# Another order of work, keys turned by 128-key block, and expert numbers cast on VectorE, in an attention, MLP and mixture-of-experts kernel

## The chip, the cores and the metric

The kernel runs on one core of a Trainium2 chip. The metric is the device time of one execution in microseconds (us), taken as the median of several runs. The engines have these names in the rows: PE (TensorE, matmuls), PEld (its weight loads), DVE (VectorE), ACT (ScalarE), POOL (GpSimd) and SP (SyncE, which issues most of the DMAs).

## The reference

Three stages follow one another; each takes the output of the one before.

1. Attention in chunks: 4 batches, 8 heads, 768 positions, head size 64. Each chunk of 32 queries sees 8 memory keys, 16 keys to the left, its own 32 and 8 to the right: 64 keys in all.
2. A dense layer on the 3072 tokens: `h = x @ w_in` (512 to 2048), `g = h * tanh(softplus(h))`, `g @ w_out` (2048 to 512).
3. A mixture of 8 experts: each token goes to the one expert whose embedding is the nearest by cosine, and gets `gate * (relu(x @ w1[e]) @ w2[e])`, with 1024 inner columns.

```python
scores = scale * np.matmul(q_c, k_full.transpose(0, 1, 3, 2))
out[:, :, c_start:c_end] = np.matmul(a, v_full)
...
g = h * np.tanh(sp)
return (g @ w_out).astype(np.float32)
...
expert_idx = np.argmax(logits, axis=1)
h = np.maximum(x[mask] @ w1[e], 0.0)
out[mask] = gate_w[mask, None] * (h @ w2[e])
```

## The kernel before, in words

**Matmuls.** Each fp32 product is split into a high and a low part and takes three matmuls (high by high, low by high, high by low). Splitting costs one cast (helper `split`, whose copy is recorded at L334) and one subtraction.

**The plan.** Nothing is issued where it is written. Every piece of work is a job of a list scheduler, `Plan`: a job names the engines that may do it with a modelled time (`on`), what it comes after (`after`), the buffers that it takes or uses (`get`, `use`) and a rank; the table NUDGE (L102) shifts the ranks of whole kinds of jobs. The plan then writes one instruction stream per engine, and each engine works through its own strictly in that order. So a stream is fixed before the launch, and an instruction that has to wait holds back all that stands behind it on its engine.

**Attention** works on 24 pairs of 64-query blocks, 6 pairs per batch. A pair P loads its queries (`load_q`) and its keys in two pieces: `load_k1` (104 rows: 8 memory keys and 96 keys) and `load_k2` (72 rows), both through helper `dma` (L319) on SP. `turn` (L511) transposes them on PE, 4 matmuls for each of the queries (128 rows, p_qT), the first key piece (104 rows, p_kT) and the second (72 rows, p_k). The copies `kT(0)` and `kT(1)` then lay the turned keys out as 4 chunks of 64 keys in a tile kT (5 copies in all, on ScalarE or VectorE). `S_` (L554, L559) multiplies them with the queries, then come the softmax, its transposition PT (L602) and the product with the values (p_X, L621).

**The dense layer** runs beside attention, since it needs only finished tokens: 128 steps, each a `p_h` of 12 matmuls (L732) and a `p_y` of 9 (L778). Attention's small PE jobs stand between these. The activation takes a chain of ScalarE and VectorE operations per step (L736 to L769).

**The experts.** `routing` works in two groups: group 1 takes the first 21 tiles of 128 tokens, while the dense layer still runs; group 2 takes the rest. A group gives tables of token places (p_tab, L1218), from which come the gather indices `gi` (L1232) and scatter indices, and the list of the expert numbers `ef`, in fp32. `numbers` (L1175) casts that list to integers, `ei`, on GpSimd, after the first two gathers of the group (L1288, issued on GpSimd too). Units of 256 tokens (pairs) or 128 (singles) then follow: units 0 to 2 are group 1's, the others group 2's. For each unit SP reads its expert's number into a register (L1302, and L1304 for the flag that says whether the weights must be fetched) and issues 8 weight loads of 512 KB (L1314): 4 of w1, then 4 of w2. The loads are split into ehi and elo; the gathered tokens are turned (`x_T`, L1331) and split into xs; `p_h` (L1395, 24 matmuls for each of the 4 chunks of a pair), the rectifier (hh), `p_y` (L1485), a scale and a scatter (L1511) end the unit. The weight tiles are two sets, used by units in turn.

Two lines set what the loads wait for:

```python
job(("experts", g), numbers, {G: 200}, rank=rk, after=[ex] + [("issue", "gather", first, a) for a in range(2)])
...
after = [("experts", g)] + ([("slo", u - 2, second, c)] if u >= 2 else [])
```

Nothing sets the order between the loads of one unit and those of the next but their ranks.

Of the kernel before, what the change touches and what calls it, by code (L numbers as in the profile page):

```python
# [38 lines left out]
HALF = KFF // 2  # L39
LEAVE = 2  # L40
# [46 lines left out]
def between(a, b):  # L87
# [15 lines left out]
    acta0=-0.6, acta1=-1.74, acta2=50.36, actb0=-1.76, actb1=-96.54, actb2=-81.79, actb3=-42.59, att00=40.88,  # L103
    att01=6.03, att02=-14.41, att03=12.63, att04=-3.12, att05=6.33, att06=-6.99, att07=-18.03, att10=10.46, att11=7.93,
    att12=-2.03, att13=-0.28, att14=-5.39, att15=28.34, att16=0.19, att17=-11.65, att20=7.04, att21=-2.49, att22=6.84,
    att23=0.68, att25=11.02, att26=-13.24, att27=2.06, att30=-0.41, att31=-70.31, att32=-0.58, att33=-1.39,
    att35=-0.38, att36=-1.67, att37=-67.52, att40=0.45, att41=-0.43, att42=13.06, att43=-2.17, att44=-38.4,
    att45=12.86, att46=9, att47=-2.37, att50=-1.08, att51=-18.11, att52=-6.46, att53=252.42, att54=-0.22, att55=-3.21,
    att56=-1.09, att57=2.56, att60=-5.29, att61=2.16, att63=-69, att64=-3.49, att65=145.06, att66=-0.33, att67=-14.14,
    att70=-0.37, att71=-329.92, att72=0.25, att73=-193.55, att74=-10.54, att75=-2.18, att76=-1.27, e00=-1.37, e01=8.52,  # L110
    e10=3.1, e11=23.17, e20=-86.99, e21=1, e30=0.07, e31=1.64, e40=10.43, e41=28.57, e50=1.56, e51=-2.1, e60=-22.39,
    e61=17.86, e70=-0.44, e71=-5.41, em=3.37, en0=24.71, en1=-0.52, en2=4.38, en3=27.95, en4=-27.14, en5=-7.94,
# [168 lines left out]
def attn_moe_moe_kernel(ctx, tc, q, k, v, mem_k, mem_v, w_in, w_out, emb, tau, w1, w2, cst, out, ydbg=None):  # L281
# [143 lines left out]
    def pairs(P):  # L425
# [39 lines left out]
        def load_k1(e):  # L465
# [5 lines left out]
            if spare or i == 0:  # L471
                dma(e, t[0:NMEM], mem_k[b].rearrange("h p d -> p h d"))
# [34 lines left out]
        def turn(name, src, rows):  # L507
            def f(e):
# [6 lines left out]
                if name == "kT":  # L515
                    tl["kT", P] = own(ktt, [128, J, 4, SEEN], "kT", bufs=1)
# [1130 lines left out]
```

## Time and profile before

| what | value |
|---|---|
| median of 3 runs | 1021.76 us (1020.55 to 1022.34) |
| the profiled execution | 1021.15 us |
| its span, first to last instruction | 1019.4 us |
| mean granted TensorE clock | 0.991 of full |
| instructions in the trace | 22817 |

The span is cut off at the first and last instruction, so the profiled execution's own time is 1.75 us longer. In a timeline or a chain each row begins with a time in us from the start of the span. A bracket at a row's end gives the idle time of its engine before it, and what ended that. A row of a chain says what the end waited for at that time. The tile names stand as out<-in.

### The profile page before, as it was taken

How to read it: one execution, taken by the hardware profiler on the slowest of the kernel's cores; microseconds unless marked ns; L12 is line 12 of the kernel's file. 1: busy time of each engine (PE TensorE's matmuls, PEld its weight loads, DVE VectorE, ACT ScalarE, POOL GpSimd, SP SyncE). 2: the span in 40 equal slices, each digit the busy share in tenths (PEclk: the TensorE clock that was granted, in tenths of full speed). 3: DMA queues.
4: the chain of work that ended last, by engine and by line, in shares of the span. 5: the costliest groups of instructions: out<-in, count | busy, mean ns of one | idle time of the engine just before them, and what ended most of it. 6: DMA issues, size and time to landing. Idle time of an engine off the chain costs nothing.

```text
span 1019.4 us, 22817 instructions
## 1 busy us (share of the span) xinstructions
PE 991.5 (97%) x8575; PEld 879.2 (86%) x8575; DVE 809.0 (79%) x1799; ACT 648.8 (64%) x1534; POOL 189.5 (19%) x142
## 2 busy tenths in 40 slices
PE   7899999999999999999999999999989999999997
PEld 6678888898888888888888899888979988988986
DVE  4889999669899869769869867979948667777972
ACT  4788888776877777778777767757424334443431
POOL 5000100000000000000000000011136455555742
PEclk9989999999999999999999999999989999999999
DMA  9997661233645234325313100089089868467300
GB/s 181 253 237 200 168 184 45 59 128 97 184 132 135 74 78 134 84 46 145 84 25 122 30 20 20 1 272 327 32 279 371 280 229 296 150 218 246 127 29 23
DMA packets 171817, 146.36 MB, mean 144 GB/s; under 512 B 105114, under 2 KB 134410, under 8 KB 171444
## 3 DMA queue, kind: packets, MB, share of 16 engines
q1 hardware_dynamic: 164868, 128.53, 43.5%
q0 software_dynamic: 5104, 15.89, 4.6%
q8 instruction: 69, 1.13, 0.5%
q10 hardware_dynamic: 1728, 0.43, 0.3%
q14 instruction: 48, 0.39, 0.1%
HBM read 137.11 MB, written 16.53 MB: 151 GB/s over the span
## 4 chain that ended last, share of the span: by engine, by line
PE 76%; DVE 8%; DMA 7%; issue 5%; POOL 2%; SPq 1%; ACT 0%; POOLq 0%; DVEq 0%
PE p_h L732 23%; PE p_y L778 23%; PE p_y L1485 10%; PE p_h L1395 9%; DMA eraw<-in_moe_w_dram 2%; PE p_h L1429 2%; DMA kn<-in_k_dram 2%; PE p_X L621 2%; PE p_S L559 2%; POOL elo L1367 1%; SPq L319 1%; PE p_PT L602 1%; PE p_xT L1331 1%; PE p_qT L511 1%; DMA qn<-in_q_dram 1%
## 5 line engine op out<-in xcount | busy, mean ns | idle before, releaser
L732 PE MATMUL p_h<-xt,win_h 128*128 128x384 f32 x1024 | 268.9, 344 | 0.6 <-DVE rn L761 0.5
L732 PEld LDWEIGHTS p_h<-xt,win_h 128*128 128x128 f32 x1024 | 185.3, 191 | 10.2 <-DVE rn L761 1.8
L732 PE MATMUL p_h<-xt,win_l 128*128 128x384 f32 x512 | 173.9, 340 | 0.0
L334 ACT CAST ehi<-eraw 128x1024 fp32r<-128x1024 f32 x89 | 92.9, 1049 | 120.0 <-PE p_y L1485 67.7
L778 PE MATMUL p_y<-wout_h,gh 128*128 128x512 f32 x384 | 157.1, 409 | 0.0
L778 PE MATMUL p_y<-wout_h,gl 128*128 128x512 f32 x384 | 151.9, 396 | 0.0
L778 PE MATMUL p_y<-wout_l,gh 128*128 128x512 f32 x384 | 151.8, 395 | 0.0
L1367 DVE TENSOR_TENSOR elo<-eraw,ehi 128x1024 fp32r<-128x1024 f32 x89 | 127.9, 1444 | 28.3 <-ACT ehi L334 27.7
L1485 PE MATMUL p_y<-ehi,hh 128*128 128x512 f32 x432 | 144.1, 400 | 0.0
L1395 PE MATMUL p_h<-xs,ehi 128*128 128x256 f32 x704 | 128.3, 283 | 7.0 <-DVE xs L1348 2.5
L755 ACT ACTIVATE m<-m,cf 128x384 f32<-128x384 f32 x128 | 79.1, 618 | 70.6 <-DVE m L751 69.7
L1395 PEld LDWEIGHTS p_h<-xs,ehi 128*128 128x128 f32 x704 | 110.4, 191 | 10.3 <-DVE xs L1348 2.7
L1367 POOL TENSOR_TENSOR elo<-eraw,ehi 128x1024 fp32r<-128x1024 f32 x39 | 94.9, 2432 | 81.1 <-DVE ehi L334 36.6
L851 DVE SCALAR_TENSOR_TENSOR junk<-ysb,en 128x512 f32<-128x512 f32 x144 | 99.0, 688 | 3.0 <-DMA ysb<-y_d 2.7
L1395 PE MATMUL p_h<-xs,elo 128*128 128x256 f32 x352 | 99.3, 282 | 0.0
L732 PEld LDWEIGHTS p_h<-xt,win_l 128*128 128x128 f32 x512 | 97.4, 190 | 0.0
L1485 PEld LDWEIGHTS p_y<-ehi,hh 128*128 128x128 f32 x432 | 80.9, 188 | 18.2 <-DVE hh L1454 0.3
L751 DVE SCALAR_TENSOR_TENSOR m<-sq,rn 128x384 f32<-128x384 f32 x128 | 71.0, 555 | 31.1 <-ACT rn L324 29.8
L758 DVE SCALAR_TENSOR_TENSOR rn<-m,rn 128x384 f32<-128x384 f32 x128 | 71.5, 558 | 30.0 <-ACT m L755 27.9
L736 ACT ACTIVATE sq<-p_h 128x384 f32<-128x384 f32 x128 | 62.8, 491 | 41.2 <-PE p_h L732 40.8
L778 PEld LDWEIGHTS p_y<-wout_h,gl 128*128 128x128 f32 x384 | 72.2, 188 | 17.3
L1485 PE MATMUL p_y<-elo,hh 128*128 128x512 f32 x216 | 85.2, 394 | 0.0
(264 smaller groups left out, 1770.8 us busy)
## 6 DMA issues: line engine op xcount, KB each, us to landing
eraw<-in_moe_w_dram SPq DMA_DIRECT2D x128, 512.0 KB
en<-en_d SPq DMA_DIRECT2D x48, 256.0 KB
vn<-in_v_dram SPq DMA_DIRECT2D x162, 56.0 KB
raw<-in_moe_w_in_dram SPq DMA_DIRECT2D x16, 512.0 KB
raw<-in_moe_w_out_dram SPq DMA_DIRECT2D x16, 512.0 KB
y_d<-ysb SPq DMA_DIRECT2D x24, 256.0 KB
qn<-in_q_dram SPq DMA_DIRECT2D x22, 256.0 KB
ysb<-y_d SPq DMA_DIRECT2D x18, 256.0 KB
```

Source lines behind the costliest of these rows:

```text
L334: (nc.scalar.copy if e == A else nc.vector.tensor_copy)(out, src)
L559: nc.tensor.matmul(ps[s][r:r + CHUNK, h, n // 2, :], a[64 * s:64 * s + 64, n, QB * h + CHUNK * x:QB * h + CHUNK * x + CHUNK], c[64 * s:64 ...
L732: nc.tensor.matmul(p, w, xt[j][:, a, kk, :], start=(n == 0), stop=(n == len(ops) - 1))
L736: nc.scalar.activation(t, tl["h", s], AF.Tanh, scale=0.5)
L751: nc.vector.scalar_tensor_tensor(t, tl["sq", s], 4.0, tl["rn", s], ALU.add, ALU.mult)
L755: nc.scalar.activation(t, t, AF.Square, bias=c15)
L758: nc.vector.scalar_tensor_tensor(tl["rn", s], tl["m", s], 0.75, tl["rn", s], ALU.add, ALU.mult)
L778: nc.tensor.matmul(yp[yh][t], x[:, c], w[g][:, o, :], start=(first and n == 0), stop=(final and n == 2))
L851: nc.vector.scalar_tensor_tensor(junk, tl["yio", t][:, 1], 1.0, tl["en", j, x], ALU.mult, ALU.mult, accum_out=lg[:, i, x:x + 1])
L1367: engs[e].tensor_sub(tl["elo", j], raw[b, second, c], tl["ehi", j].bitcast(F32))
L1395: nc.tensor.matmul(p[:, o, :], w[:, kk, s], v[:, kk, :], start=(kk == 0 and m == 0), stop=(kk == KDM - 1 and m == 2))
L1485: nc.tensor.matmul(tl["yy", u][a], v[:, kk, s], w[:, k, :], start=(kk == 0 and m == 0), stop=(kk == KEF - 1 and m == 2))
```

## The change

- **Keys.** From pair 6 on (`CARRY = 6`) a pair loads only its 128 new keys, in one piece, and turns them in one go of 128 rows. The 24 first keys of its window (8 of memory, 16 of the left) are kept: `keep` copies the last 16 from the previous pair's kT tile, which is now one tile for all; the first pair of a batch (6, 12, 18) loads 24 rows and turns these apart. `fresh_keys` lays out the rest with 2 copies. All of these, the turn too, come after `S` of the previous pair.
- **Expert numbers.** `numbers` runs on VectorE, and no longer after the group's first gathers.
- **Loads.** A unit's first weight load is issued after the last one of the unit before it.
- **Order.** NUDGE has new values, so that all work but the first loads and projections stands in another order.

By instructions: the turns p_k of 72 rows go from 96 matmuls to 24 and those of 104 rows from 88 to 16; 72 of 128 rows and 12 of 32 rows are new. Everything else on PE keeps its count. The new numbers of NUDGE are cut here to a line or two.

```diff
--- before.py
+++ after.py
...
+CARRY = 6
...
 NUDGE = dict(
-    acta0=-0.6, acta1=-1.74, acta2=50.36, actb0=-1.76, actb1=-96.54, actb2=-81.79, actb3=-42.59, att00=40.88,
...
+    acta0=-0.6, acta1=-1.51, acta2=-13.73, acta3=-199.64, actb0=-1.9, actb1=-983.54, actb2=-220.88, actb3=-519.98,
...
+        carry, start = P >= CARRY, P >= CARRY and i == 0
+        KB = NMEM + PREV
...
+            if carry:
+                get_keys(e, t, 0, w + PREV, w + PREV + 2 * QB)
+                return
...
+            if carry:
+                dma(e, t[0:NMEM], mem_k[b].rearrange("h p d -> p h d"))
+                get_keys(e, t, NMEM, w, w + PREV)
+                return
...
-                if name == "kT":
+                if name == "kT" and not carry:
...
+        def keep(e):
+            if P == CARRY:
+                tl["kTs"] = own(ktt, [128, J, 4, SEEN], "kT", bufs=1)
+            t = tl["kT", P] = tl["kTs"]
+            if i == 0:
+                p = tl["T", "k2", P]
+                copy(e, t[:, :, 0, 0:KB], p)
+                x = p[:, :, 0:NMEM]
+                copy(e, t[:, :, 1:4, 0:NMEM], bass.AP(tensor=x.tensor, offset=x.offset, ap=[x.ap[0], x.ap[1], [0, 3], x.ap[2]]))
+            else:
+                copy(e, t[:, :, 0, NMEM:KB], t[:, :, 3, SEEN - PREV:])
+
+        def fresh_keys(e):
+            t, p = tl["kT", P], tl["T", "kT", P]
+            copy(e, t[:, :, :, KB:], p.rearrange("p j (c n) -> p j c n", c=4))
+            x = p[:, :, CHUNK - PREV:CHUNK]
+            copy(e, t[:, :, 1:4, NMEM:KB], bass.AP(tensor=x.tensor, offset=x.offset, ap=[x.ap[0], x.ap[1], [CHUNK, 3], x.ap[2]]))
...
+            if start:
+                plan.dma(("k2", P), load_k2, size=rows(KB), rank=L(0.05), after=[("issue", "q", P)], get=[(k2t, k2s)], **iss(2))
+            plan.dma(("k1", P), load_k1, size=rows(128), rank=L(0.1), after=[("issue", "k2" if start else "q", P)], get=[("kn", ks)], **iss(2 if i == NQB - 2 else 1))
...
-        qh, kt, xb = ("qT", P), ("kT", P), [("X", P, a) for a in range(2)]
...
-        job(("Tk", P, 0), turn("kT", "kn", K1), {E: 350}, rank=R(0), after=[("k1", P)], use=[kh], get=[("a", t2), (ktt, kt)])
-        job(("Tk", P, 1), turn("k2", "kn2", K2), {E: 250}, rank=R(0), after=[("k2", P)], use=[k2s], get=[("a", t3)])
...
+        else:
+            if start:
+                job(("Tk", P, 1), turn("k2", "kn2", KB), {E: 290}, rank=R(0), after=[("k2", P), ("S", P - 1)], use=[k2s], get=[("a", t3)])
+            job(("Tk", P, 0), turn("kT", "kn", 128), {E: 436}, rank=R(0), after=[("k1", P), ("S", P - 1)], use=[kh], get=[("a", t2)])
...
+        if not carry:
+            job(("kT", P, 0), kT(0), {A: 750, V_: 900}, rank=R(1), after=[("Tk", P, 0)], use=[t2, kt])
+            job(("kT", P, 1), kT(1), {A: 430, V_: 530}, rank=R(1), after=[("Tk", P, 1)], use=[t3, kt])
+        else:
+            job(("kT", P, 1), keep, {A: 420, V_: 400} if start else {A: 160, V_: 115, G: 250}, rank=R(1), after=[("S", P - 1)] + ([("Tk", P, 1)] if start else [("kT", P - 1, 0)]),
+                get=[(ktt, kt)] if P == CARRY else [], use=([t3] if start else []) + ([] if P == CARRY else [kt]))
+            job(("kT", P, 0), fresh_keys, {A: 830, V_: 1000}, rank=R(1), after=[("Tk", P, 0), ("kT", P, 1), ("S", P - 1)], use=[t2, kt])
...
                 c = slice(first, u1 if g == 1 else NUNIT)
-                nc.gpsimd.tensor_copy(ei[:, c], ef[:, c])
-
-            job(("experts", g), numbers, {G: 200}, rank=rk, after=[ex] + [("issue", "gather", first, a) for a in range(2)])
+                nc.vector.tensor_copy(ei[:, c], ef[:, c])
+
+            job(("experts", g), numbers, {V_: 80}, rank=rk, after=[ex])
...
                 after = [("experts", g)] + ([("slo", u - 2, second, c)] if u >= 2 else [])
+                if u and c == 0 and second == 0:
+                    after.append(("issue", "ld", u - 1, 1, NC_ - 1))
...
-                put_job(("ld", u, second, c), load(second, c), dict(SP=470), base - 7 + 1.5 * second + 0.3 * c, after,
+                put_job(("ld", u, second, c), load(second, c), dict(SP=470 + (0 if c or second else 950 if u < 2 else 1450)), base - 7 + 1.5 * second + 0.3 * c, after,
                         [(f"w{8 * b + 4 * second + c}", h)] if u < 2 else [], [] if u < 2 else [h], dma=2 ** 19)
```

Three places in the streams follow. In the changed kernel, lines stand 2 to 46 further down: L511 is L522, L559 is L588, L732 is L776, L778 is L822, L1175 is L1219, L1288 is L1332, L1314 is L1358.

**PE, a pair in the middle of attention.** p_qT, p_kT and p_k are the turns of the queries and of the keys; the rows of p_h and p_y belong to the dense layer. Before, two turns of keys stand apart, each between a `p_h` and a `p_y`:

```order
L732 MATMUL p_h<-xt,win_h 128x384 x2
L732 MATMUL p_h<-xt,win_l 128x384
L511 MATMUL p_kT<-cf,kn 128x104 x4
L778 MATMUL p_y_6604<-wout_h,gh 128x512
...
L511 MATMUL p_k_7188<-cf,kn 128x72 x4
L778 MATMUL p_y_6604<-wout_h,gh 128x512
L778 MATMUL p_y_6604<-wout_l,gh 128x512
```

After, one turn of 128 rows follows directly on the previous pair's S:

```order
L588 MATMUL p_S<-kT,qT 32x64 x32
L522 MATMUL p_kT<-cf,kn 128x128 x4
L822 MATMUL p_y_6576<-wout_h,gh 128x512
...
L822 MATMUL p_y_6578<-wout_h,gl 128x512
L522 MATMUL p_qT<-cf,qn 128x128 x4
L776 MATMUL p_h<-xt,win_h 128x384 x2
```

The second key turn (72 rows) is gone, and the first now has 128 rows and stands behind S instead of behind a `p_h`.

**POOL and VectorE, the expert numbers.** vn are the gathered tokens, ei the integer numbers, out_dram<-yo the scatters. Before, on POOL, both casts stand behind gathers:

```order
L594 TENSOR_TENSOR pr<-pr,sm 128x256 x5
L1288 DMA vn<-y_d,gi 128x512 x2
L1175 CAST ei<-ef 1x3
L1288 DMA vn<-y_d,gi 128x512 x4
L1511 DMA out_dram<-yo,si 3072x512 x4
L1288 DMA vn<-y_d,gi 128x512 x2
L1175 CAST ei<-ef 1x20
L1367 TENSOR_TENSOR elo<-eraw,ehi 128x1024
```

After, on VectorE, the second group's cast stands directly behind the last step of the list (ra<-ra 1x3), ahead of the places' copy (ra<-p_tab) and of gi:

```order
L1252 TENSOR_TENSOR rhs_9581<-rhs_9581,ra 128x3x32
L1210 TENSOR_TENSOR ra<-ra 1x1
L1252 TENSOR_TENSOR rhs_9585<-rhs_9585,ra 128x3x32
L1211 CAST ra<-ra 1x3
L1252 TENSOR_TENSOR rhs_9587<-rhs_9587,ra 128x3x32
L1219 CAST ei<-ef 1x20
L1274 COPY ra<-p_tab 128x96
L1252 TENSOR_TENSOR rhs_9589<-rhs_9589,ra 128x3x32
L1275 SCALAR_TENSOR_TENSOR ra<-ra 128x32
L1413 TENSOR_TENSOR elo<-eraw,ehi 128x1024
L1276 CAST gi<-ra 128x32
```

The cast moved from behind four scatters and two gathers on POOL to the end of the list's own arithmetic on VectorE.

**SP, the first expert loads.** `TENSOR_LOAD ei` begins a unit; loads from w1 are the chunks that `p_h` needs, loads from w2 those of `p_y`. Rows of register moves (ISA) are left out at the dots. Before, the second unit begins behind one load of the first, and the two take turns (eraw_9093, 9108, 9144 and 9166 are the first unit's, the others the second's):

```order
L1314 DMA eraw_9093<-in_moe2_w1_dram 128x4x256
L1302 TENSOR_LOAD ei_102
...
L1314 DMA eraw_9106<-in_moe2_w1_dram 128x4x256
...
L1314 DMA eraw_9108<-in_moe2_w1_dram 128x4x256
...
L1314 DMA eraw_9133<-in_moe2_w1_dram 128x4x256
...
L1314 DMA eraw_9144<-in_moe2_w1_dram 128x4x256
...
L1314 DMA eraw_9164<-in_moe2_w1_dram 128x4x256
...
L1314 DMA eraw_9166<-in_moe2_w1_dram 128x4x256
...
L1314 DMA eraw_9169<-in_moe2_w1_dram 128x4x256
```

After, the first unit's eight loads stand together, w1 and then w2, ahead of the second unit's:

```order
L1346 TENSOR_LOAD ei_102
...
L1358 DMA eraw_8742<-in_moe2_w1_dram 128x4x256
...
L1358 DMA eraw_8773<-in_moe2_w1_dram 128x4x256
...
L1358 DMA eraw_8789<-in_moe2_w1_dram 128x4x256
...
L1358 DMA eraw_8796<-in_moe2_w1_dram 128x4x256
...
L1358 DMA eraw_8801<-in_moe2_w2_dram 128x2x512
...
L1358 DMA eraw_8806<-in_moe2_w2_dram 128x2x512
...
L1358 DMA eraw_8823<-in_moe2_w2_dram 128x2x512
...
L1358 DMA eraw_8831<-in_moe2_w2_dram 128x2x512
L1346 TENSOR_LOAD ei_102
```

The first unit's fourth w1 chunk was the seventh load from its start and is now the fourth. The same holds for unit 3, the first of group 2. Two more moves on PE belong to this place: unit 0's turned tokens (x_T) now stand 3 `p_h` and 3 `p_y` of the dense layer behind the first tables, and the 96 matmuls of its first `p_h` stand in four parts between the last `p_y` of the dense layer, where three parts stood together before. Unit 3's x_T stands two chunks of `p_y` (24 matmuls) nearer to group 2's tables than before.

## Rows read from the trace of the kernel before

**Rows 1.** the page: busy time, share of the span and instructions of each engine

```profile
PE 991.5 (97%) x8575; PEld 879.2 (86%) x8575; DVE 809.0 (79%) x1799; ACT 648.8 (64%) x1534; POOL 189.5 (19%) x142
```

**Rows 2.** windows: us, busy (count) of PE, PEld, DVE, ACT, POOL; PEclk, DMA share, GB/s

```profile
120.00:140.00 20.00, 20.00 (x225) 17.63 (x223) 20.00 (x46) 16.25 (x43) 1.31 (x1) 1.00 0.66 177
...
675.00:685.00 10.00, 8.17 (x65) 7.66 (x64) 6.68 (x9) 5.12 (x8) 0.00 (x0) 1.00 1.08 359
...
755.00:765.00 10.00, 5.55 (x25) 4.91 (x24) 4.91 (x6) 3.65 (x5) 5.38 (x5) 0.69 1.06 375
```

**Rows 3.** chain of waits, one pair's steps: start us, length us, piece

```profile
496.70 0.44 PE p_qT L511 x4
497.13 2.08 PE p_h L732 x12
499.22 0.36 PE p_kT L511 x4
499.58 2.12 PE p_y L778 x9
...
503.78 0.25 PE p_k L511 x4
504.03 2.14 PE p_y L778 x9
...
508.69 2.10 PE p_y L778 x9
```

**Rows 4.** groups by form, weight loads of the 72-row turns: ns min/median/max

```profile
L511 PEld LDWEIGHTS p_k<-cf,kn x96: 138/139/230, 6.8 to 528.5; 72*128 72x128 f32 x96
```

**Rows 5.** chain of waits, 671 to 719 us, the first expert unit

```profile
671.39 9.06 DMA eraw<-in_moe_w_dram
...
683.44 3.09 PE p_h L1395 x24
...
688.64 2.83 PE p_h L1395 x24
...
707.80 11.30 PE p_h L1395 x96
```

**Rows 6.** timeline of PE: start, length, operation, idle before it and its releaser

```profile
680.33 0.36 PE L1395 MATMUL p_h<-xs,ehi 128*128 128x256 f32 x1 [1.78 <-DVE rn L761]
...
757.51 0.38 PE L1395 MATMUL p_h<-xs,ehi 128*128 128x256 f32 x1 [1.90 <-ACT xs L334]
760.44 0.58 PE L1395 MATMUL p_h<-xs,ehi 128*128 128x256 f32 x1 [2.55 <-DVE xs L1348]
```

**Rows 7.** timeline of POOL: the two casts of expert numbers

```profile
666.59 0.58 POOL L1175 CAST ei<-ef 1x3 int32<-1x3 f32 x1
...
742.16 0.19 POOL L1175 CAST ei<-ef 1x20 int32<-1x20 f32 x1
```

**Rows 8.** timeline of DVE: the last step of the second group's expert numbers

```profile
734.02 0.15 DVE L1167 CAST ra<-ra 1x3 int32<-1x3 f32 x1
```

**Rows 9.** chain of waits, 743 to 774 us, the first unit of group 2

```profile
743.83 3.40 DMA eraw<-in_moe_w_dram
...
749.92 9.15 DMA eraw<-in_moe_w_dram
...
760.44 13.77 PE p_h L1395 x95
```

**Rows 10.** timeline of PE, then the chain, at 110 us: a wait on key copies

```profile
110.39 1.09 PE L602 MATMUL p_PT<-cf,pr 128*128 128x128 f32 x4 [1.36 <-DVE kT L334]
...
111.47 3.15 PE p_h L732 x12
```

**Rows 11.** chain of waits, 51 us: a key load beside other loads

```profile
51.59 8.92 DMA kn<-in_k_dram
```

**Rows 12.** chain of waits, 831 us: a gather beside expert loads

```profile
831.64 4.19 DMA vn<-y_d,gi
```

More of the change, by code (lines that the diff above doesn't have):

```diff
@@ L108 @@
[L108 to L112, printed above, removed]
@@ new lines @@
+    e01=-32.25, e10=43.46, e11=465.55, e20=203.75, e21=-11.76, e30=-6.98, e40=38.85, e41=18.19, e51=-9.73, e60=15.22,
+    e61=-34.22, e70=19.91, e71=0.58, em=-116.42, en0=64.17, en1=-2.77, en2=21.77, en3=62.78, en4=-34.11, en5=-0.65,
+    hh0=-0.66, hh1=-8.88, hh2=2.85, ld00=-35.58, ld01=62.6, ld10=39.27, load0=8.15, load1=17.34, load10=-1.5,
+    load11=22.13, load2=-45.54, load3=-3.15, load4=-2.18, load5=-0.64, load7=3.07, load9=4.58, mm_y0=12.67,
+    mm_y1=223.46, mm_y2=1.17, mm_y3=-0.1, out0False=-84.93, out0True=450.72, out1False=-12.91, out2False=112.15,
@@ L120 @@
+    raw0=-8.26, raw1=5.15, raw10=465.44, raw11=121.43, raw2=-9.44, raw3=-3.37, raw4=-0.07, raw5=-13.38, raw6=29.5,
+    raw7=26.79, raw9=-0.21, route=0.73, rows0=-82.55, rows1=-125.79, rows2=-32.63, split0=0.59, split10=298.76,
+    split11=-7.41, split3=-2.85, split4=-6.67, split5=17.18, split6=129.33, split9=99.19, xs0=-1.01, xs1=0.03,
+    xs2=-91.69, ye1=-2.5, ye2=-14.75, ye3=69.58, ye4=-0.87, ye5=-27.9, yre0=49.56, yre1=-1.9, yre3=-29.93, yre4=6.6,
+    yre5=9.41,
 )
@@ L638, in pairs @@
         qs, ks, k2s = ("qn", P), ("kn", P), ("kn2", P)
-        plan.dma(("q", P), load_q, size=rows(128), rank=L(0), after=[("issue", "k2", P - 1)] if P else [], get=[(qkt[0], qs)], **iss(1))
-        plan.dma(("k1", P), load_k1, size=rows(K1), rank=L(0.1), after=[("issue", "q", P)] if P > 1 else [("issue", "k1", 0)] if P else [], get=[] if spare else [("kn", ks)], use=[qs] if spare else [], **iss(3 if i == 0 else 2 if spare else 1, A if P < 2 else "SP"))
-        plan.dma(("k2", P), load_k2, size=rows(K2), rank=L(0.2), after=[("issue", "q" if P < 2 else "k1", P)], get=[(k2t, k2s)], **iss(2 if i == NQB - 2 else 1))
+        plan.dma(("q", P), load_q, size=rows(128), rank=L(0), after=([("issue", "k1" if P > CARRY else "k2", P - 1)] if P else []), get=[(qkt[0], qs)], **iss(1))
+        if not carry:
+            plan.dma(("k1", P), load_k1, size=rows(K1), rank=L(0.1), after=[("issue", "q", P)] if P > 1 else [("issue", "k1", 0)] if P else [], get=[] if spare else [("kn", ks)], use=[qs] if spare else [], **iss(3 if i == 0 else 2 if spare else 1, A if P < 2 else "SP"))
+            plan.dma(("k2", P), load_k2, size=rows(K2), rank=L(0.2), after=[("issue", "q" if P < 2 else "k1", P)], get=[(k2t, k2s)], **iss(2 if i == NQB - 2 else 1))
+        else:
+            if start:
+                plan.dma(("k2", P), load_k2, size=rows(KB), rank=L(0.05), after=[("issue", "q", P)], get=[(k2t, k2s)], **iss(2))
+            plan.dma(("k1", P), load_k1, size=rows(128), rank=L(0.1), after=[("issue", "k2" if start else "q", P)], get=[("kn", ks)], **iss(2 if i == NQB - 2 else 1))
         kh = qs if spare else ks
@@ L651, in pairs @@
         mxh, sm = (pr, pr) if spare else (("mx", P), ("sm", P))
-        qh, kt, xb = ("qT", P), ("kT", P), [("X", P, a) for a in range(2)]
+        qh, kt, xb = ("qT", P), ("kT", min(P, CARRY)), [("X", P, a) for a in range(2)]
         mems = spare or i == 0
```

25 lines of the change are left out of this document (12 added, 13 removed).

## The prediction

> **What bounds the kernel now.** I read the page first. PE is busy for 991.5 of 1019.4 us [rows 1], so the whole kernel is one long queue of matmuls, and only two things can shorten it: less work on PE, or less waiting of PE. All its waiting together is some 28 us. Then I read the windows, to find where that waiting lies. In the middle PE is full even where VectorE is full too: 20.00 of 20.00 us each from 120 to 140 us [rows 2]. The reader is to see in that row that VectorE at 100% costs PE nothing there. The windows with holes are those in which the experts begin: 8.17 of 10 us from 675 to 685, and 5.55 of 10 from 755 to 765, where the granted clock also falls to 0.69 of full, that is, between the two levels of 1.2 and 2.4 GHz [rows 2]. PE's timeline gives the holes their sizes, 1.78, 1.90 and 2.55 us, and the chains of waits their causes [rows 5, 6, 9]: transfers of expert weights that end last.
>
> **The change part by part.**
>
> *a) Turns of keys.* In an ordinary pair the chain shows both key turns on PE's path: 0.36 us for 104 rows and 0.25 us for 72. The `p_y` behind each takes 2.12 and 2.14 us where 2.10 is usual, so both together cost 0.36 + 0.25 + 0.02 + 0.04 = 0.67 us [rows 3]. The new turn has the shape of the queries' turn, 0.44 us [rows 3]. That is 0.23 us less for each of 15 ordinary pairs from the seventh on, 3.45 us. The three pairs that begin a batch keep a second turn of 32 rows. By the step from 72 to 104 rows (0.11 us for 32) and the 0.04 of the following `p_y` I estimate 0.15 us for it: 0.44 + 0.15 against 0.67, 0.08 less, 0.24 us for the three. Together **-3.7 us**. The bounds: 0, if the new neighbours (S directly before the turn) cost what is saved; and -8.3 us, if PE pays each of the 4 fewer weight loads per pair in full, 4 x 0.139 us x 15 [rows 4]. I take the chain's figure, because 4 transpositions of 72 rows took 0.25 us there, 0.06 each, less than half the duration of the weight load of one: the loads overlap.
>
> On the weight loads the Trainium skill has a rule ("TensorE: Matmul & The Clock Gate", section "LDWEIGHTS (loading the stationary operand)"): their time goes by columns and not by rows of contraction. By it a turn of 72 rows would cost as much as one of 128, and a pair would save 4 whole loads; the sum by it is the -8.3 us above in place of -3.7. The trace agrees on the loads themselves (138 to 139 ns even at 72 rows), but the chain charges PE for rows.
>
> The copies of keys go from 5 to 3 per pair, on ScalarE and VectorE, which PE does not wait for in mid-attention [rows 2]; nothing. They now come after the previous pair's S, and the pair's S after them, but between the two lie five dense steps in mid-attention, 5 x (2.08 + 2.10) = 21 us [rows 3].
>
> *b) The first expert unit.* PE waited 1.78 us before its `p_h`, whose first chunk then took 3.09 us against 2.83 for a later one [rows 5, 6]. It waited for the weight transfer of 9.06 us [rows 5] with the queues full (359 GB/s) [rows 2]. Two units' loads took turns, so the first unit's fourth chunk was the seventh transfer; now it is the fourth. Three transfers of 0.524 MB at 375 GB/s [rows 2] are 4.2 us, over twice the wait. The cast no longer stands behind gathers on POOL either, where it ran at 666.59 us and took 0.58 [rows 7]. The wait goes: 1.78 + 0.26 = **-2.0 us**.
>
> *c) The first unit of group 2.* The cast of 20 numbers ran at 742.16 us [rows 7], though their arithmetic ended at 734.02 + 0.15 = 734.17 [rows 8]: eight us behind gathers and scatters. Only then could SP read the number and begin the load at 743.83, whose successors ended with one of 9.15 us [rows 9]. PE waited 1.90 + 2.55 = 4.45 us [rows 6], and then ran the 95 matmuls of `p_h` in 13.77 us at a low clock, where 96 took 11.30 [rows 5, 9], so 11.18 for 95: 2.59 lost. The change brings the start 8 us forward and the fourth chunk another 4.2, together 12 against 4.45 needed. With the wait goes the low clock that followed it: 4.45 + 2.59 = **-7.0 us**. The cast itself costs VectorE about 0.15 us, like the cast of rows 8, beside PE's work. What is queued behind it there, the indices, waits for that long only. SP's register loads now hold back the following unit's loads until the 8 before are issued; since those are needed first, nothing.
>
> *d) The stretch from 60 to 130 us,* where pairs 6 to 8 follow each other at a distance of about one dense step. There the transposition PT waited 1.36 us behind VectorE's key copies, and the `p_h` after it took 3.15 against 2.08 [rows 3, 10]; both could go (-2.4), or return at another copy. I take 0, with +5.8 as the other bound (rival 2).
>
> Everything else moves without losing or gaining instructions. The copies, casts and products that change sides between VectorE, ScalarE and POOL have PE's full queue as cover; if it were gone in some stretch, VectorE's long operations there would show as gaps of half a us each.
>
> Sum: -3.7 - 2.0 - 7.0 = -12.7, against the profiled execution's own 1021.15 us: 1008.45. The median of the runs stands 0.61 us above that execution, so **1009.0 us**.
>
> **The rivals.**
>
> *Rival 1, the gathers of unit 3 are the new wait.* Its turned tokens stand two chunks of `p_y` (2 x 2.8 us, by the size of a `p_h` chunk [rows 5]) nearer to the tables than before, and a gather took 4.19 us beside expert loads [rows 12]. Now the loads start before the gathers. Between 0 and 5.6 us come back; I take 3: 1012. For it: both holes of 1.90 and 2.55 us end with xs, the turned tokens' copies [rows 6]. Against it: the gathers no longer queue behind the cast. Chance 0.15.
>
> *Rival 2, keys late for pairs 7 and 8.* One tile holds the natural keys, so the next load begins after the turn before; the two turns stand about 6 us apart (one `p_h`, one `p_y`, an S, a queries' turn). A key load took 8.92 us beside other loads [rows 11], and it is now one of 256 KB. Two gaps of 2.9 us are 5.8: 1014.8. Against it: later the transfers are fewer, and the 8.92 was in the crowded beginning. Chance 0.10.
>
> *Rival 3, PE pays each weight load,* the -8.3 us of part a: 1004.4. For it: each of those loads has a row of its own, as long at 72 rows as at any [rows 4]. Against it: the chain's short turns. Chance 0.04.
>
> *Rival 4, slower: unit 0's gathers queue behind the weights.* Sixteen loads, 8.4 MB, are now issued close to its gathers. At 375 GB/s [rows 2] they take 22.4 us. The turned tokens stand 3 `p_h` and 3 `p_y` behind the tables, 3 x (2.08 + 2.10) = 12.5 us [rows 3]. If the gathered rows came only behind all weights, and then took 4.19 us [rows 12], PE would wait 22.4 + 4.2 - 12.5 = 14.1 us, and lose another 2.6 to the clock as in part c: 1025.7. It decides from the point at which the gather lands over 12.5 us after the tables. Against it: the gather at 831.64 us shared the queues with weights and landed in 4.19 [rows 12]. Chance 0.06.
>
> On that the Trainium skill ("DMA: Bandwidth & Descriptors", section "Queues, rings and completion order") says that each DMA engine goes round the queues that have work, packet by packet, so that a gather shares rather than queues. It speaks against rival 4, and the gather at 831.64 us agrees; by it rival 4 would have no chance at all.
>
> *Rival 5, the change does not do what it says:* the casts come earlier, but VectorE's splits of the chunks, with the routing's small operations between them, end as late as the transfers did, and the turns' gain goes into the S before them. Then the time stays, about 1021. Against it: VectorE was busy for 4.91 of 10 us in the window of the wait [rows 2]. Chance 0.06.
>
> **How the numbers follow.** The forecast has 0.59, the rivals 0.15, 0.10, 0.04, 0.06 and 0.06. The range starts at 1002.5: about the forecast with part a at its other end (-4.6) and part d at its own (-2.4), 1002.0. It ends at 1016.5, past rivals 1 and 2 and short of both at full price; rivals 4 and 5 stay outside, 0.12. A measurement of this kernel tells about 0.2%, 2 us, from no change. Faster by more: the forecast and rivals 1 to 3, 0.88; same, rival 5, 0.06; slower, rival 4, 0.06.
>
> **What would show it.** Part a: one 128-row turn in a pair's chain, near 0.44 us, no second one. Part b and c: windows at both beginnings of the experts with PE at 10.00 of 10 us and PEclk 1.00; the cast on VectorE right behind the list's end; the next weight loads issued within 2 us of it. Rival 1 would show as a wait for vn before p_xT or for xs near group 2's start, rival 2 as one for kn before p_kT between 60 and 130 us, rival 4 as one over 10 us before unit 0's p_xT, rival 5 as one for elo or ehi. The prediction is wrong if the holes stay as long with another releaser, or if attention's stretch gains more than 6 us or loses more than 4.

## The result, and the profile after

The changed kernel takes 1009.5 us (median of 4 runs, 1008.56 to 1009.97) where the kernel before took 1021.15 beside it: a ratio of 0.9885, with a 95% interval of 0.9868 to 0.9902. The forecast was 1009.0. The profiled execution's span is 12.7 us shorter (1006.7 against 1019.4), as the sum of the prediction had it; its parts were not all of the size forecast.

The page after, to set beside [rows 1]:

```profile
span 1006.7 us, 22780 instructions
...
PE 985.0 (98%) x8515; PEld 874.1 (87%) x8515; DVE 789.6 (78%) x1766; ACT 662.3 (66%) x1536; POOL 192.5 (19%) x140
```

PE is busy for 6.5 us less and waits for 6.2 us less (21.7 against 27.9). Windows of 10 us at the beginning of the experts, with the columns of [rows 2]:

```profile
670.00:680.00 10.00, 9.24 (x64) 8.25 (x63) 6.42 (x9) 4.93 (x7) 0.00 (x0) 1.00 1.06 357
690.00:700.00 10.00, 10.00 (x42) 7.78 (x42) 6.82 (x30) 4.84 (x8) 1.69 (x2) 0.84 0.19 54
750.00:760.00 10.00, 10.00 (x84) 9.86 (x83) 5.28 (x7) 4.62 (x7) 4.78 (x4) 1.00 1.07 371
```

The windows are those of three events: the first expert unit, the expert work that follows it, and the first unit of group 2. In the last, where PE was busy for 5.55 of 10 us before, it now is for all 10 at the full clock. The middle row was not forecast: PE never idles there, and yet the granted clock is 0.84. At the first it still waits, in PE's timeline, for 0.76 us:

```profile
671.94 0.51 PE L1441 MATMUL p_h<-xs,ehi 128*128 128x256 f32 x2 [0.76 <-DVE rn L805]
```

What releases the weights, in SP's timeline of the changed kernel, each row a run of transfers:

```profile
642.00 34.31 SPq L1358 DMA_DIRECT2D eraw<-in_moe_w_dram  x23
...
720.10 26.53 SPq L1358 DMA_DIRECT2D eraw<-in_moe_w_dram  x19
```

in that of the kernel before, where the first run began:

```profile
668.31 24.51 SPq L1314 DMA_DIRECT2D eraw<-in_moe_w_dram  x19
```

and in VectorE's of the changed kernel, the list's last step and the cast:

```profile
718.23 0.15 DVE L1211 CAST ra<-ra 1x3 int32<-1x3 f32 x1
...
718.46 0.16 DVE L1219 CAST ei<-ef 1x20 int32<-1x20 f32 x1
```

The cast follows its list at once and the weights follow the cast by 1.5 us. The first transfers are 26 us earlier than before (642.0 against 668.3), of which about 20 are the first tables' (PE's p_tab at 640.94 against 660.88), which now stand 41 us ahead of the dense layer's end.

| part | forecast, us | from the rows, us | from what |
|---|---|---|---|
| a) key turns | -3.7 | -4.1 | rows of a pair, below |
| b) first expert unit | -2.0 | -1.0 | 0.76 of idle PE left of 1.83 (670 to 690 us) |
| c) first unit of group 2 | -7.0 | -7.0 | both holes and the low clock gone |
| d) 60 to 140 us | 0 | -1.5 | below |
| clock at 690 us | not named | +1.5 | 12 matmuls of p_y in 4.43 us for 2.88 |
| the rest | 0 | -0.6 | what is left of 12.7 |

In d the wait of [rows 10] is gone, with its slow `p_h`. PE's idle time from 60 to 140 us falls only from 2.91 to 2.47 us, because a shorter wait stands nearly in its place, 0.80 us before the `p_h` at 109.63 us, for the dense layer's own activation (VectorE's rn).

### The profile page after: what moved, and what is told of

Same layout as the page of the kernel before. It is cut to its first block, busy times and chain, and to the rows that moved or that the text cites. A ratio compares the mean times of both kernels' runs of the same rounds, so it can differ in the third digit from the quotient of the medians.

```text
span 1006.7 us, 22780 instructions
## 1 busy us (share of the span) xinstructions
PE 985.0 (98%) x8515; PEld 874.1 (87%) x8515; DVE 789.6 (78%) x1766; ACT 662.3 (66%) x1536; POOL 192.5 (19%) x140
## 5 line engine op out<-in xcount | busy, mean ns | idle before, releaser
L776 PE MATMUL p_h<-xt,win_h 128*128 128x384 f32 x1024 | 268.1, 343 | 1.1 <-DVE rn L805 1.1
L776 PEld LDWEIGHTS p_h<-xt,win_h 128*128 128x128 f32 x1024 | 184.2, 190 | 9.8 <-DVE rn L805 2.7
L776 PE MATMUL p_h<-xt,win_l 128*128 128x384 f32 x512 | 173.2, 338 | 0.0
L822 PE MATMUL p_y<-wout_h,gh 128*128 128x512 f32 x384 | 154.6, 403 | 0.0
L822 PE MATMUL p_y<-wout_l,gh 128*128 128x512 f32 x384 | 152.0, 396 | 0.0
L822 PE MATMUL p_y<-wout_h,gl 128*128 128x512 f32 x384 | 151.9, 396 | 0.0
L1413 DVE TENSOR_TENSOR elo<-eraw,ehi 128x1024 fp32r<-128x1024 f32 x89 | 119.4, 1348 | 31.7 <-ACT ehi L336 30.0
L1441 PE MATMUL p_h<-xs,ehi 128*128 128x256 f32 x704 | 125.2, 279 | 0.8 <-DVE rn L805 0.8
L776 PEld LDWEIGHTS p_h<-xt,win_l 128*128 128x128 f32 x512 | 97.0, 189 | 0.0
L822 PEld LDWEIGHTS p_y<-wout_h,gl 128*128 128x128 f32 x384 | 72.2, 188 | 17.1
```

What stands on the lines that cost most here:

```text
L776: nc.tensor.matmul(p, w, xt[j][:, a, kk, :], start=(n == 0), stop=(n == len(ops) - 1))
L822: nc.tensor.matmul(yp[yh][t], x[:, c], w[g][:, o, :], start=(first and n == 0), stop=(final and n == 2))
L1413: engs[e].tensor_sub(tl["elo", j], raw[b, second, c], tl["ehi", j].bitcast(F32))
L1441: nc.tensor.matmul(p[:, o, :], w[:, kk, s], v[:, kk, :], start=(kk == 0 and m == 0), stop=(kk == KDM - 1 and m == 2))
```

## The experiments

Each kernel ran beside the kernel before on the same chip. Since chips differ by a few us, the ratios to the kernel before are compared. The changed kernel's is 0.9885, and 0.9891 when it ran again. A trace is of one execution only: waits of 1.7 to 2.5 us for a gather between 830 and 940 us stand in three of the traces below (1.95 us at 830.53 with the turn made twice, 1.74 at 937.78 with the loads' old order, 2.45 at 939.45 with the logits apart) and not in the changed kernel's first one.

### The turns of the keys

**No carry:** two turns per pair again.

```diff
-CARRY = 6
+CARRY = 24
```

> The changed kernel with two key turns per pair as before (104 and 72 rows), everything else as changed. Theory A (the turns are worth what the rows of PE show): in the changed kernel S, turn and the dense p_y behind them take 0.81 + 0.42 + 2.18 = 3.41 us where S and p_y alone took 3.08 before, so a pair pays 0.33 for its turn instead of 0.67; undone, 15 x 0.34 + 3 x 0.2 = 5.7 us come back: 1015 (by the prediction's own 3.7: 1013). Rival: the fall of PE's busy time came from the clock alone and the turn gains nothing: 1009.5, within 1 us.

Measured: 1012.53 us, ratio 0.9918 (0.9899 to 0.9938), 3 us over the changed kernel with some 2.5 us of uncertainty, nearer to the prediction's own 3.7 than to theory A's 5.7. PE's timeline in this kernel:

```profile
494.97 0.52 PE L522 MATMUL p_kT<-cf,kn 104*128 104x104 f32 x4
495.26 0.48 PE L822 MATMUL p_y<-wout_h,gh 128*128 128x512 f32 x1
...
499.53 0.41 PE L522 MATMUL p_k<-cf,kn 72*128 72x72 f32 x4
499.75 0.48 PE L822 MATMUL p_y<-wout_h,gh 128*128 128x512 f32 x1
```

The start of one row to the start of the next is what PE spends on it: 0.29 to 0.30 us for 104 rows and 0.22 for 72 rows. Each `p_y` behind a turn starts with a matmul that takes 0.08 us longer than usual: 0.30 + 0.22 + 0.16 = 0.68 us per pair. In the changed kernel the same rows are:

```profile
486.97 0.88 PE L588 MATMUL p_S<-kT,qT 64*32 64x64 f32 x64
487.78 0.66 PE L522 MATMUL p_kT<-cf,kn 128*128 128x128 f32 x4
488.20 0.48 PE L822 MATMUL p_y<-wout_h,gh 128*128 128x512 f32 x1
```

The turn takes 0.42 us and the `p_y` behind it the same 0.08 more; but a `p_y` behind S alone also takes 0.10 more. So the new turn costs PE 0.42, and saves 0.26 per pair, 3.9 us in 15, with 0.2 for the batch starts 4.1. By PE's groups the key turns are busy for 19.4 us instead of 23.7, 4.3 less, which agrees.

**Turn twice:** 4 more transpositions per pair, no other change of order.

```diff
-                for n in range(J):
+                for n in [*range(J)] * (2 if carry and name == "kT" else 1):
                     nc.tensor.transpose(p[:, n, :], ...
```

> The changed kernel with the 128-row turn of the keys made twice in each of the 18 pairs from the seventh on (4 more transpositions into the same place), all streams otherwise in the same order. By the chain's price of the prediction, 0.44 us for a turn of 128 rows: 18 x 0.44 = 7.9 us more, 1017.4. If PE paid the weight loads in full (0.14 us each): 18 x 0.56 = 10, 1019.6. If a turn behind S costs what the changed kernel's rows say (3.41 against 3.08 us): 18 x 0.33 = 5.9, 1015.4.

Measured: 1017.74 us, ratio 0.9951 (0.9933 to 0.9968), 6 us over the changed kernel's ratio, with some 3 us of uncertainty. PE's timeline:

```profile
494.74 1.10 PE L522 MATMUL p_kT<-cf,kn 128*128 128x128 f32 x8
495.59 0.48 PE L822 MATMUL p_y<-wout_h,gh 128*128 128x512 f32 x1
```

Eight transpositions take 0.85 us (494.74 to 495.59), four more for 0.43: the chain's price of 0.44 was right, 18 x 0.43 = 7.7 us. Weight loads paid in full (0.56 per turn, 10 us) are excluded, by these rows and, narrowly, by the time. The Trainium skill ("TensorE: Matmul & The Clock Gate", section "LDWEIGHTS (loading the stationary operand)") counts a load by its columns; the rows of weight loads agree [rows 4], but four of them overlapped with the matmuls so far that a transposition cost 0.11 us, less than its load of 0.139.

### The cast and the order between the loads

**Both back to the old,** in the changed kernel (and SP's modelled time).

```diff
-nc.vector.tensor_copy(ei[:, c], ef[:, c])
+nc.gpsimd.tensor_copy(ei[:, c], ef[:, c])
...
-job(("experts", g), numbers, {V_: 80}, rank=rk, after=[ex])
+job(("experts", g), numbers, {G: 200}, rank=rk, after=[ex] + [("issue", "gather", first, a) for a in range(2)])
...
-                if u and c == 0 and second == 0:
-                    after.append(("issue", "ld", u - 1, 1, NC_ - 1))
```

> The changed kernel with the cast of expert numbers back on GpSimd behind the gathers and without the order between the units' weight loads; new NUDGE and new turns stay. Theory A (the casts and the loads' order took the two stalls away): both come back, 1.1 + 4.45 + 2.6 us, about 1017.5. Rival (the new order of work did it: the first tables stand 41 us ahead of the dense layer's end instead of 26, and group 2's first unit has 34 us after its tables): the weights are early in any case, 1009.5 to 1011, with no wait over 1 us at either beginning.

Measured: 1020.44 us, ratio 0.999 (0.9966 to 1.0014). Nearly the whole gain is gone, and PE's timeline shows both waits:

```profile
676.34 0.80 PE L1439 MATMUL p_h<-xs,ehi 128*128 128x256 f32 x2 [4.34 <-DVE hh L1456]
...
744.36 0.47 PE L1439 MATMUL p_h<-xs,ehi 128*128 128x256 f32 x2 [3.60 <-DVE hh L1456]
```

So the new order by itself did not take the waits away.

**The order between the loads alone,** in the kernel before (the two lines above with a plus, and SP's modelled time).

> The kernel before with one part of the change alone: a unit's weight loads follow all of the unit before it (and its modelled time for SP's register load). Theory A: the fourth chunk is the fourth transfer instead of the seventh, 4.2 us earlier at both places, the first stall of 1.83 goes, the second shrinks from 4.45 to some 0.3 and its slow clock goes: 1021.2 - 2.0 - 6.7 = 1012.5. Rival (only the cast's place counts in group 2): -2 alone, 1019.

Measured: 1019.11 us, ratio 0.9979 (0.9965 to 0.9994). The second wait is gone, as theory A had it; but the first has grown from 1.78 to 5.59 us:

```profile
683.94 0.77 PE L1397 MATMUL p_h<-xs,ehi 128*128 128x256 f32 x2 [5.59 <-DVE rn L761]
```

So the time is the rival's 1019, by another way than the rival's.

**The cast alone back,** in the changed kernel (the first four lines above).

> The changed kernel with the cast of expert numbers alone back on GpSimd behind the gathers; the order between the units' loads stays. Theory D (a stall comes when a weight transfer ends late and ScalarE's split of it, which waits, stands ahead of work that PE needs; the start of the loads counts, and in group 2 the cast sets it, 15 us after the tables instead of 2): the first place stays clear, since the loads in unit order give the fourth chunk by about 658 us and PE needs it from 666 us on; in the second place the stall of 3.6 us and some 0.9 of slow clock come back: 1014. Rival (the loads' order alone cures both, as it did the second place in the kernel before): 1009.5 to 1010.5.

Measured: 1017.88 us, ratio 0.9964 (0.9946 to 0.9982); its profiled execution took 1012.98, the shortest of the ten. The first wait is 1.17 us, the second is back:

```profile
737.30 0.76 PE L1441 MATMUL p_h<-xs,ehi 128*128 128x256 f32 x2 [3.76 <-DVE hh L1458]
```

Theory D's place was right, and in this trace the size of the wait (3.76 us for 3.6). The median is 4 us beyond its 1014, which this trace of the shortest execution does not explain.

**The loads' order alone back.** Its edit is the last two lines of the first diff, and SP's modelled time.

> The changed kernel without the order between the units' loads, the cast staying on VectorE. Theory D: the loads start at 642 and 720 us as in the changed kernel, the first unit's fourth chunk is the seventh transfer again and lands by about 655 us, 11 us before PE begins with it, so nothing comes back: 1009.5 to 1010.5. Rival (both parts are needed, each cures one of the two places): the first stall comes back with about 4.3 us, 1014.

Measured: 1012.97 us (1008.13 to 1016.84), ratio 0.9899 (0.9855 to 0.9943). The second place is clear, and the first waits:

```profile
677.48 0.51 PE L1439 MATMUL p_h<-xs,ehi 128*128 128x256 f32 x2 [2.59 <-DVE rn L805]
```

The interval holds both no change and 5 us. The trace speaks for the first place alone: 2.59 us there instead of 0.76. So by these two traces, in the new order the earlier cast cured group 2, and the loads' order helps the first unit; that the latter is worth time is not shown.

### What PE waited for

The rows of the waits name VectorE's rn and hh, and in group 2 of the kernel before the turned tokens xs [rows 6], not weights. In the kernel before, at the first wait, ScalarE's timeline reads:

```profile
676.82 1.05 ACT L334 CAST ehi<-eraw 128x1024 fp32r<-128x1024 f32 x1 [1.82 <-DMA eraw<-in_moe_w_dram]
677.78 0.61 ACT L755 ACTIVATE m<-m,cf 128x384 f32<-128x384 f32 x1
```

The split of weights (ehi) waited 1.82 us for its transfer, and the activation m of the dense layer's last step stood behind it. VectorE's timeline has the same once more, with the second half of the split (elo) ahead of rn, which needs m:

```profile
677.90 1.23 DVE L1367 TENSOR_TENSOR elo<-eraw,ehi 128x1024 fp32r<-128x1024 f32 x1 [2.31 <-ACT ehi L334]
679.05 0.55 DVE L758 SCALAR_TENSOR_TENSOR rn<-m,rn 128x384 f32<-128x384 f32 x1
```

A second rn, 0.58 us behind the first, ends the activation and frees the PSUM buffer into which the next `p_h` goes. That `p_h`'s own weights were split at 679.13 us and PE was free from 678.55, so they alone explain 0.6 of the 1.78 us. In the kernel with the loads' order alone the plan had put two more splits ahead of m, since it took the weights for early:

```profile
679.96 1.04 ACT L334 CAST ehi<-eraw 128x1024 fp32r<-128x1024 f32 x1 [1.23 <-DMA eraw<-in_moe_w_dram]
680.91 0.61 ACT L755 ACTIVATE m<-m,cf 128x384 f32<-128x384 f32 x1
```

There m came 3.1 us later (680.91 against 677.78), and PE went on 3.6 us later (683.94 against 680.33).

In group 2 of the kernel before, PE had turned the tokens by 752.8 us, and their copies (xs) stood behind splits of later chunks, first on ScalarE, then on VectorE:

```profile
755.44 1.04 ACT L334 CAST ehi<-eraw 128x1024 fp32r<-128x1024 f32 x1 [7.14 <-DMA eraw<-in_moe_w_dram]
756.39 1.07 ACT L334 CAST xs<-p_xT 128x512 fp32r<-128x512 f32 x2
...
759.10 0.69 DVE L334 CAST ehi<-eraw 128x1024 fp32r<-128x1024 f32 x1 [0.75 <-DMA eraw<-in_moe_w_dram]
759.70 0.68 DVE L1348 TENSOR_TENSOR xs<-p_xT,xs 128x512 fp32r<-128x512 f32 x1
```

The first chunk's own weights had been split at 749.6 us, 8 us before PE began with them. So the 4.45 us of part c, too, were spent on what stood behind the splits; that copies ahead of the splits would have saved them in the kernel before is argued here, not tried.

With the cast alone back, it is the rectifier hh of unit 2 that stands behind unit 3's first split:

```profile
734.25 1.04 ACT L336 CAST ehi<-eraw 128x1024 fp32r<-128x1024 f32 x1 [7.51 <-DMA eraw<-in_moe_w_dram]
735.20 0.59 ACT L1450 ACTIVATE hh<-p_h 128x512 fp32r<-128x512 f32 x1
```

**Theory F: the rectifier first.** To test it, the split was only put behind that rectifier; the cast stayed late.

```diff
-... rk, [("ld", u, second, c)] + ([("shi", u - 1, second, c)] if u else []), ...
+... rk, [("ld", u, second, c)] + ([("shi", u - 1, second, c)] if u else []) + ([("hlo", 2, 3)] if main and u == 3 and not second else []), ...
```

> The experiment with the cast back on GpSimd, and one thing added: unit 3's splits of w1 come after the rectifier of unit 2's last chunk, so ScalarE no longer stands in front of that rectifier waiting for unit 3's first weights (7.5 us there). Theory F (PE's wait of 3.76 us was for a PSUM buffer, whose rectifier stood behind a split that waited for weights; PE needed the weights themselves only 15 us later): that wait goes, though the weights come as late as before, 4 to 8 us less than the run with the cast alone, about 0.990 of before. Rival (the weights themselves are late for unit 3): the wait moves to unit 3's first p_h and stays 3 us or more.

Measured: 1012.77 us, ratio 0.9911 (0.9888 to 0.9933). On ScalarE all four rectifiers of unit 2 now pass on time, and the splits follow:

```profile
736.30 0.60 ACT L1450 ACTIVATE hh<-p_h 128x512 fp32r<-128x512 f32 x1 [2.23 <-PE p_h L1441]
...
739.63 1.04 ACT L336 CAST ehi<-eraw 128x1024 fp32r<-128x1024 f32 x1
```

The wait of 3.76 us is gone. Another turns up at unit 3's own first `p_h`, 16 us later, for the turned tokens:

```profile
753.59 0.38 PE L1441 MATMUL p_h<-xs,ehi 128*128 128x256 f32 x1 [2.30 <-DVE xs L1394]
```

So the rival's wait came in part, but not for late weights of that `p_h`. VectorE's xs stood behind an ehi that had waited 2.77 us for its transfer, and behind three elo that took 7.90 us, where one takes 1.22, while GpSimd ran two elo of its own:

```profile
744.44 7.90 DVE L1413 TENSOR_TENSOR elo<-eraw,ehi 128x1024 fp32r<-128x1024 f32 x3
752.26 1.27 DVE L1394 TENSOR_TENSOR xs<-p_xT,xs 128x512 fp32r<-128x512 f32 x2
...
745.38 5.88 POOL L1413 TENSOR_TENSOR elo<-eraw,ehi 128x1024 fp32r<-128x1024 f32 x2
```

Theory F holds for the wait of 3.76 us. By the medians, putting one dependence right won 5 us (0.9964 to 0.9911) without touching the late cast. The two traces do not show that gain: their executions took 1012.98 us, the shortest with the cast back, and 1013.86 us here. What made the other executions with the late cast longer stays open.

### The order of work

**The new NUDGE alone,** in the kernel before.

> The kernel before with the new NUDGE alone: old turns, old cast, no order between loads. Theory E (the new order gains nothing by itself; its worth is that it fits the early weights): both stalls as in the experiment without the new cast and loads, and 3 us more for the turns: 1020 to 1024, 0.999 to 1.003 of before. Rival (the order is the main gain): below 1016.

Measured: 1025.19 us, ratio 1.004 (1.0024 to 1.0057): slower than before. Both waits stand there:

```profile
680.57 0.50 PE L1396 MATMUL p_h<-xs,ehi 128*128 128x256 f32 x2 [3.60 <-DVE hh L1413]
...
749.51 0.48 PE L1396 MATMUL p_h<-xs,ehi 128*128 128x256 f32 x2 [3.42 <-DVE hh L1413]
```

**The old NUDGE,** with all the rest of the change.

> The changed kernel with the old NUDGE: new turns, cast and loads in the old order of work. Theory E: like the kernel before with cast and loads (1.005 of before, two waits of 4.5 us), less 3 to 4 us for the turns: 1.001 of before, 1022 to 1025. Rival (the turns' move makes the schedule fit again): near 1010.

Measured: 1046.48 us, ratio 1.0243 (1.0221 to 1.0264), far beyond either theory. The page's row of granted clocks:

```profile
PEclk9989987999999999999999999989999999999999
```

The waits are no longer two. They stand from 112 to 175 us too, with 4.17 us at 163.76 as the longest there, and that is where the digits 8 and 7 stand side by side. Another is 5.04 us long, where ScalarE's gh is late for a `p_y` at the dense layer's end (PE's timeline):

```profile
699.93 0.80 PE L821 MATMUL p_y<-wout_h,gh 128*128 128x512 f32 x1 [5.04 <-ACT gh L335]
```

Here the old order meets turns that it was not made for, so the loss is that of the combination.

**Cast and loads in the kernel before,** old turns and old NUDGE.

> The kernel before with the cast on VectorE and the order between the loads, old NUDGE and old turns. Theory D: the loads start early and in order, both stalls go: 1021.5 - 1.8 - 7.0 = 1012.7. Rival (the new NUDGE is needed, because the old one orders the splits on ScalarE and VectorE for late weights): one stall stays, 1015 to 1019.

Measured: 1028.17 us, ratio 1.0048 (1.0028 to 1.0068), slower too. PE's timeline:

```profile
678.72 0.79 PE L778 MATMUL p_y<-wout_h,gh 128*128 128x512 f32 x1 [4.58 <-ACT gh L334]
...
720.17 0.58 PE L1397 MATMUL p_h<-xs,ehi 128*128 128x256 f32 x1 [4.45 <-DVE xs L1350]
```

Two waits of 4.5 us, at other places than before: at a `p_y` of the dense layer for gh, and at the second unit's `p_h` for xs. The rival is right in kind (one ehi stands directly ahead of gh on ScalarE, at 677.22 us), but it named one wait, and the price is higher than it said.

### The clock at 690 us

**The logits kept apart:** the second and third p_lg each after a chunk of an expert's p_y.

```diff
-job(k("L"), L, {E: 858}, rank=R[1], after=[k("b1"), ("em", 4)], ...
+job(k("L"), L, {E: 858}, rank=R[1], after=[k("b1"), ("em", 4)] + ([("Y", 0, n % TPB - 1)] if j == NBLK - 1 and n % TPB else []), ...
```

> The changed kernel with the three groups of small logit matmuls at the dense layer's end (p_yT, p_lg, p_xT, 5.0 us in one piece before) kept apart by chunks of an expert's p_y: two of the three p_lg come after a chunk each. Theory C (that piece of small matmuls is what the clock fell behind, to 0.50 of full from 690 to 692 us, where 12 matmuls of p_y took 4.4 us instead of 2.8): the 1.6 us come back, 1007.9, PEclk 1.00 from 680 to 710. Rival 1: the fall has another cause and stays, 1009.5. Rival 2: the second group's tables, now 5.6 us later, make PE wait in group 2's first unit, 1010 to 1013.

Measured: 1010.94 us (1008.84 to 1014.68), ratio 0.9897 (0.9875 to 0.9918): no gain. In the trace, that of the slowest of its four executions, the clock is full there now, and low at 740 us:

```profile
690.00:700.00 10.00, 10.00 (x60) 8.33 (x59) 5.94 (x17) 5.77 (x8) 1.78 (x1) 1.00 0.17 53
740.00:750.00 10.00, 7.98 (x32) 6.13 (x31) 4.79 (x6) 4.21 (x5) 4.26 (x4) 0.83 1.05 378
```

where PE waits for group 2's gathers, which follow the later tables (rival 2; PE's timeline):

```profile
742.60 0.66 PE L1377 MATMUL p_xT<-cf,vn 128*128 128x128 f32 x4 [2.02 <-DMA vn<-y_d,gi]
```

**The changed kernel again.**

> The changed kernel once more, on the same chip as the three below, as their measure. 1009.5, or about 0.9885 of the kernel before on this chip. Open: whether the fall of the clock at 690 us and the wait of 0.76 us at 672 are there again; the same piece of small matmuls went by without a fall in three experiments, so theory C expects a fall again and the rival (chance of the moment) expects none.

Measured: 1010.58 us, ratio 0.9891 (0.987 to 0.9912). The window is as in the first trace:

```profile
690.00:700.00 10.00, 10.00 (x50) 8.18 (x50) 6.64 (x29) 5.54 (x11) 1.90 (x2) 0.83 0.30 99
```

But the kernel without carry, with the same order of PE in that stretch, has

```profile
690.00:700.00 10.00, 10.00 (x66) 8.57 (x65) 7.22 (x32) 7.09 (x15) 1.90 (x2) 1.00 0.42 132
```

so the piece of small matmuls is not enough for the fall. Nor does the fall belong to the changed kernel: with the new NUDGE alone the clock is 0.50 from 699 to 702 us, in and behind the same piece. What decides it stays open.

No version beat the changed kernel: the two that come closest, with the logits apart and with the loads' old order, have medians above it and intervals that overlap its own.

## Why the prediction was right, and where it was not

**Time and sign** were right, and the likeliest case is the one that came. That the sum came out to a tenth of a us is luck: part b's missing 1.0 and the clock's 1.5 on one side met 0.4 in part a, 1.5 in part d and 0.6 of the rest on the other. Rivals 1, 2 and 4 did not show: the gathers of unit 3 landed in time, no kn wait of the changed kernel stands at a 128-row turn, and unit 0's p_xT did not wait (654.74 and 657.30 us). Rival 1 shows in the experiment with the logits apart, as a wait of 2.02 us for vn with a granted clock of 0.83 over those 10 us; the prediction had given it 0 to 5.6 us and no clock.

**Part a** was right within 0.4 us, and by its own working: 0.67 us for the two turns (0.68 in the run without carry), 0.44 for one (0.42 and 0.43). Rival 3 is excluded by the doubled turn.

**Part b** was the term that was mis-sized: "The wait goes: 1.78 + 0.26" should have been half of that. The step behind it, that PE waits for the weight transfer, was one engine short. PE waited for a PSUM buffer, which the end of the dense layer's activation frees, and that activation stood in ScalarE's and in VectorE's stream behind the split that waited for weights. The transfer of 9.06 us that the prediction named was not the one either: it ended at 680.45 us [rows 5], when PE had gone on at 680.33, and the `p_h` of 3.09 us is the second after the wait (it begins at 683.44). With early weights the late split went, and 0.76 us (0.81 in the repetition) are left in which the dense layer's last activation is itself too slow: on VectorE its m follows a split (elo) and the step before's gl, and the rn that frees the buffer follows from that m:

```profile
667.90 1.22 DVE L1413 TENSOR_TENSOR elo<-eraw,ehi 128x1024 fp32r<-128x1024 f32 x1
...
669.50 0.55 DVE L795 SCALAR_TENSOR_TENSOR m<-sq,rn 128x384 f32<-128x384 f32 x1
```

That is rival 5 in small.

**Part c** had the right size, all of it. Of its two reasons, the earlier cast is the one that counts: with the cast alone back the wait returns (3.76 us), with the loads' order alone back it does not. That the prediction added both ("8 us forward and the fourth chunk another 4.2") did no harm to the sum, since the 8 us alone were more than the 4.45 needed. Its step from the transfer to PE was short in the same way as in part b: PE waited for xs behind splits, while the weights for its first chunk had been there for 8 us.

**Part d** was taken at zero and gave 1.5 us; it lay within its bounds.

**What no step had** is that the parts hold only together. Priced one by one, the cast and the loads alone should have won about 9 us in the old order: they lost 5 (1.0048). The new order alone should have cost nothing and lost 4 (1.004), and the old order with all else lost 25 (1.0243). The prediction read the final streams, so its sum could come out; for the cast and the loads by themselves, its prices would have had the wrong sign. The turns by themselves, and the cast by itself, were not tried in the kernel before. Nor did any step have the clock's fall at 690 us (+1.5), which the gain in d made up for.

## What to carry to other kernels

Where engines work through fixed streams, a late transfer does its harm at the first instruction behind the one that waits for it: follow the releaser that the wait names back along its engine's stream to a row that waits for a DMA, and see whether that row could stand later (the experiment with the rectifier first is the one in which this was tried). A number that releases transfers (here the experts' numbers) belongs right behind its arithmetic, on an engine with nothing slow in front of it. And the parts of a change to a planned order are to be priced in the streams that the plan then makes, never by adding what each would do in the old ones.

## What the runs showed of the hardware that was not expected

**The granted clock fell without any idle time of PE.** In the two traces of the changed kernel it is 0.84 and 0.83 over 690 to 700 us, and 0.50 from 690 to 692 in the first and from 692 to 695 in the second, so the lower of the two levels of 1.2 and 2.4 GHz. PE was busy throughout, with 44 small matmuls and transpositions in 5.0 us just before (12 p_yT, 24 p_lg, 8 p_xT). With the new NUDGE alone it fell within the same 44, and in two other experiments behind 36 of that kind (0.50 from 694.5 to 697 us with cast and loads in the kernel before, and from 725 to 727.5 us with the old NUDGE). The same 44 went by at the full clock in six others: without carry, with the turn made twice, and with the old cast, the old loads' order, both, and the rectifier first.

**VectorE and GpSimd are slower beside each other.** With the cast back, group 2's second gather and the cast behind it read:

```profile
720.00 6.64 POOL L1332 DMA_INDIRECT vn<-y_d,gi  x1 [0.30 <-issue]
726.64 2.13 POOL L1219 CAST ei<-ef 1x20 int32<-1x20 f32 x1
```

where the cast took 0.19 us before [rows 7] and most gathers take about 1 us (half of the changed kernel's take 0.98 or less). VectorE was busy for 10.00 of 10 us just before and for 9.31 of 10 then. The gather is as slow in the changed kernel, only the cast no longer stands behind it:

```profile
722.34 6.65 POOL L1332 DMA_INDIRECT vn<-y_d,gi  x1 [0.31 <-issue]
```

It goes the other way too, as with the rectifier first: of VectorE's 89 elo in the changed kernel, the 74 that meet none of GpSimd's took at most 1.23 us, and the 15 that meet one took 1.26 to 3.74. The Trainium skill ("SBUF — State Buffer", section "Who interferes with whom") has the two engines share one port pair as an exclusive lock, on which a VectorE instruction with two operands in SBUF contends with a GpSimd instruction that reads SBUF. The rows of elo agree with that in kind, and those of the cast would; what holds the gather for 6.6 us is not shown, since no run here took VectorE's work away. It is one more reason why the cast is better placed on VectorE, which did it in 0.16 us.
